# A long convolution and a state-space scan on one core: the convolution's transforms in smaller array pieces, with real and imaginary part on one partition, and a new order of all queues

## The chip, the cores and the metric

The kernel runs on one core of a Trainium2 chip. The metric is the device time of one launch in microseconds (us); lower is better. The core has five engines with a queue each: TensorE (PE in the profile, with its weight loads as a row of their own, PEld), VectorE (DVE), ScalarE (ACT), GpSimd (POOL) and SyncE (SP). Here POOL and SP do little but issue DMA transfers.

## The reference, cut to what matters

All inputs are bfloat16; S = 2048 positions, D = 1024 channels, L = 2S = 4096.

```python
# half A: gated long convolution            -> out[..., 0:1024]
k_shift = sum over t<4 of k_pad[:, t:t+S, :] * shift_k[:, 3-t]
kv  = k_shift * v
y   = irfft(rfft(pad(kv, L)) * rfft(pad(ssm_k, L)))[:S]    # along positions
out_a = q * (y + kv * ssm_D)

# half B: diagonal state-space model         -> out[..., 1024:2048]
dt = exp(log_dt);  Lam_bar = exp(dt * Lam)                 # complex, 1024 states
Bu = x @ (((Lam_bar - 1)/Lam)[:, None] * B).T
h[t] = Lam_bar * h[t-1] + Bu[t]
out_b = 2 * real(h @ C.T) + x * Dskip
```

## The kernel before

Everything is written out by hand. A string `ORDER` lists some 1,200 small tasks; the loop at the end of `full_kernel` runs them in that order, so that each engine's queue holds its share of the tasks in the order of the string. A word is a task with its arguments; `:a3` names the buffer slot that its result takes, and `@G`, `@S`, `@D` put a DMA on POOL's or SP's queue or a copy on DVE. No scheduler moves anything afterwards: a task that isn't ready holds up all that stands behind it on its engine.

Half B runs in 16 chunks i of 128 positions. B is loaded in 16 pieces (`bl`), turned on TensorE (`bT`, L458) and copied to `BT` by ACT or DVE (`bc`, L473 or L469). `x` (L483) and `cx` (L480) are transposing DMAs. `U.i.jp.jl` (L492) makes Bu in 16 matmuls of 128 columns; four `ue.i.jp` (ACT, L497) copy it out. Then DVE does, per chunk: `r1` (multiply by a rotating table, L506), `r2` (add, L518), `sc` (the scan, L523), `cm` (carry to the next chunk, L528), `r3` (L506) and `r4` (L535). `y.i.dh.part` (L546, and L551 for the skip) multiplies by C; `ye` (ACT, L556) and `yst` store it.

Half A is a 4096-point transform in two stages, through DRAM between them:

- `kp`, `vp` load k and v; `kvm`, `kva`, `kvb`, `kvc` (DVE, L583 to L604) make two rows of kv at a time.
- Stage 1: a 64-point transform over 128 partitions that hold two interleaved groups of 64 positions. The matrix `F1t` is padded with zeros to 128 x 128, so `am.r.u` (L610, two matmuls of 512 columns) does one half u of the frequencies for both groups; `ae` (ACT, L615) and `ast` store to `Ys_kv`. For the filter, `hl` loads, `hT` (L630) turns eight blocks on TensorE, `hc` (L635) copies, `hm.f.rp.u` (L643) is the matmul, `he` (L650) and `hst` store to `Ys_h`.
- Stage 2, for 16 groups gq: `lh`, `lk` load 512 KB each; `sh`, `sk` (L676) are 64 x 64 pieces, four of them in the array at a time; `she`, `ske` (ACT, L685, L691) copy to `hab` and `x16`. The real part stands on one 32-partition block and the imaginary part on the next. `sw` exchanges them: four SBUF-to-SBUF DMAs of 32 partitions. Then `pr` (DVE, L704) multiplies both forms by the k side, `sa` (L717, 64 x 64 pieces again) transforms back, `sae` (ACT, L724) and `vst` store to `Vs`.
- Last stage: `vl` and `qp` load, `a3.r` (L744, four matmuls with a padded `Gt`), `a3e` (ACT, L749), `qm` (multiply by q, DVE, L753), `ost`.

PSUM is eight banks: `p0`, `p1` (one bank each) and `d0` to `d2` (two banks each). The pool `a1` (k ring, filter taps) is closed when the convolution input is done, and `a2` (slots `a11` and up, `hab`) takes its place.

Of the kernel before, what the change touches and what calls it, by code (L numbers as in the profile page):

```python
# [16 lines left out]
BF16 = mybir.dt.bfloat16  # L17
# [5 lines left out]
NR = 16  # L23
# [4 lines left out]
def a_constants():  # L28
# [3 lines left out]
    F1 = np.zeros((64, 2, 2, 2, 2, 32))  # L32
    G1 = np.zeros((2, 2, 32, 2, 64, 2))
    for h in range(2):
        F1[:, h, :, h] = np.transpose(F, (0, 2, 1, 3))
        G1[h, :, :, :, :, h] = np.transpose(F, (1, 3, 2, 0)) * (2 / NFFT)
# [5 lines left out]
    WF = np.zeros((2, N2, 2, 32, 3, N2))  # L42
# [3 lines left out]
    WF[:, :, :, :, 2, :] = WF[:, :, :, :, 0, :]  # L46
    WI = np.zeros((2, 2, N2, 16, 2, 2, N2, 2))
    for gi in range(2):
        for ui in range(2):
            for gq in range(16):  # L50
                cc = np.transpose(c_[ui, 2 * gq + gi], (1, 0)); ss = np.transpose(s_[ui, 2 * gq + gi], (1, 0))
                o = WI[gi, :, :, gq, ui]
                o[0, :, 0, :, 0] = cc; o[0, :, 0, :, 1] = ss
                o[1, :, 0, :, 0] = -cc; o[1, :, 0, :, 1] = -ss
                for cp in range(2):
                    o[cp, :, 1, :, 0] = -ss; o[cp, :, 1, :, 1] = cc
    W = np.concatenate([WF.reshape(128, NWP, 4 * 96), WI.reshape(128, NWP, 2 * 256)], axis=2)
# [9 lines left out]
ld_par bl.4.0@G:b0 bl.5.0@G:b1 bl.5.1@G:b2 bl.4.1:b3 bl.6.0:b4 bl.2.1@G:b5 ld_sd@S bl.1.1@G:b6 ld_w@S:a0a1 kp.0@G kp.-2 ld_F par_T:p0 hl.2@G:a2  # L67
bl.7.0:b7 bT.4.0:p1 p32 exp1 bl.6.1:b8 hl.3@G:a3 bc.4.0 dve2 x.0:b9 kp.-1@G bT.5.0:p0 dve3 sm_pre bT.4.1:p1 bc.5.0 hl.1@G:a4 bl.0.1:b10 bc.4.1
bl.7.1@G:b11 x.4:b12 bT.6.0:p0 tabA1:a5a6a7a8 bc.6.0 bl.2.0:b13 hl.0:a9 exp2 bl.0.0:b0 sin0 rt@G kp.1 bT.1.1:p1 x.2:b1 bT.5.1:p0 tabA2 bc.1.1 cx.4.1
wb.7:p1 bc.5.1 par_rest vp.0@G:a10 ld_G@S sin2 wb.4:p0 cx.5.1 wbe.4 sin1 wb.6:p0 cx.0.0 wbe.6@D eo.0 bl.3.1:b3 wb.1:p0 wbe.7@D bl.1.0:b4 wbe.1@D  # L70
wb.2:p1 cx.0.1 eo.1 stt.0 wb.0:p0 cx.7.0 wbe.2 stt.1 eo.3 wb.5:p1 bl.3.0:b6 x.1:b2 wbe.5@D wbe.0 stt.3 wb.3:p1 wbe.3 bT.6.1:p0 cx.1.0 dd bT.2.0:p1
kvm.0:m0 vp.1:a1 vp.2:a0 cx.6.0 bc.6.1 cx.6.1 bT.0.1:p0 bc.2.0 bc.0.1@D kp.2@G eo.2 bT.2.1:p1 kva.0 hT.0.0:p0 hc.0.0:b8 stt.2 bc.2.1 hT.0.1:p0
bT.7.1:p1 hc.0.1:b13 kvb.0:a7 bc.7.1 hT.0.6:p0 hm.0.0.1:d0 kvc.0 hc.0.6:b10 hT.0.3:p1 hm.0.0.0:d1 kvm.4:m0 he.0.0.1:b5 am.1.1:d2 hc.0.3:b11
hm.0.6.1:d0 hst.0.0.1 hT.0.2:p0 bT.0.0:p1 he.0.6.1:b8 hc.0.2:b0 hst.0.6.1@S cx.1.1 bc.0.0 bT.7.0:p0 bc.7.0@D cx.3.1 z1 U.0.3.0:p1 kva.4 hm.0.6.0:d0
U.0.3.1 cx.3.0 U.0.2.0:p0 kvb.4:a8 U.0.2.1 ue.0.3:a10 he.0.6.0:b7 kvm.2:m0 bT.1.0:p1 bc.1.0 am.0.1:d0 bT.3.0:p1 ue.0.2 bc.3.0 bT.3.1:p0 bc.3.1
U.0.0.0:p1 U.0.0.1 he.0.0.0:b5 kp.4@G kva.2 kp.3@G ae.0.1:b10 hm.0.3.1:d1 U.2.2.0:p0 ue.0.0 ast.0.1@S vp.4:a5 kvc.4 U.0.1.0:p1 ae.1.1:b4 cx.5.0
hm.0.1.0:d0 he.0.3.1:b6 ast.1.1 kvb.2:a6 hm.0.3.0:d2 hst.0.6.0 U.0.1.1 he.0.1.0:b3 hst.0.3.1 kvc.2 U.2.2.1 ue.0.1 hst.0.1.0 he.0.3.0:b11 U.1.2.0:p1
r1.0:m0 ue.2.2:a0 hst.0.3.0@S hm.0.1.1:d1 hst.0.0.0@S am.4.0:d0 he.0.1.1:b8 cx.2.0 U.2.1.0:p0 r2.0:a1 U.1.2.1 U.2.1.1 ue.1.2:a10 kvm.8:m0 U.1.1.0:p1
ue.2.1 ae.4.0:b13 hm.0.2.0:d2 am.4.1:d1 z2 ast.4.0 am.0.0:d0 U.2.3.0:p0 hst.0.1.1 ae.4.1:b4 U.1.1.1 he.0.2.0:b7 ast.4.1@S sc.0 U.2.3.1 ue.1.1
hst.0.2.0@S hm.0.2.1:d1 cx.7.1 ue.2.3 am.5.1:d2 ae.0.0:b6 hT.0.4:p1 cx.2.1 am.2.0:d0 hc.0.4:b10 ast.0.0 U.1.0.0:p0 ae.2.0:b3 hT.0.7:p1 cx.4.0 kva.8  # L80
U.1.0.1 ue.1.0 hT.0.5:p0 hc.0.7:b0 hl.5:a9 kvb.8:a4 hl.4:a2 U.2.0.0:p1 hc.0.5:b13 ast.2.0@S hl.7:a3 r3.0:m0 U.1.3.0:p0 he.0.2.1:b8 am.1.0:d0 hst.0.2.1
hm.0.5.0:d1 U.1.3.1 cm.0:a7 kvc.8 U.2.0.1 ue.1.3 he.0.5.0:b11 r4.0 U.4.0.0:p0 ue.2.0 hm.0.4.0:d1 r1.1:m0 U.4.0.1 he.0.4.0:b5 U.4.2.0:p1 ue.4.0:a5
hst.0.4.0@S ae.5.1:b6 hm.0.7.1:d1 r2.1 U.4.2.1 ae.1.0:b4 ast.5.1 U.4.1.0:p0 hl.6@G:a10 r1.2:m0 he.0.7.1:b7 ast.1.0@S hst.0.5.0 am.8.1:d2 ue.4.2
U.4.1.1 hm.0.5.1:d0 sc.1 am.5.0:d1 he.0.5.1:b8 U.4.3.0:p1 ue.4.1 am.2.1:d0 ae.5.0:b3 y.0.0.0:p0 ae.2.1:b13 hm.0.4.1:d1 hm.0.7.0:d0 ast.2.1@S U.4.3.1
x.3:b6 he.0.7.0:b10 r2.2:a0 am.8.0:d0 ae.8.1:b5 hst.0.7.0 y.0.0.1 r3.1:m0 hst.0.5.1 ue.4.3 ast.8.1@S ast.5.0@S y.0.0.2 ae.8.0:b0 vp.3:a8 y.0.1.0:p1
ast.8.0 cm.1 hst.0.7.1 r4.1 am.3.0:d2 y.0.1.1 ae.3.0:b4 r1.4:m0 y.0.0.3 ast.3.0 ye.0.0:b11 hT.1.4:p0 y.0.1.2 sc.2 hc.1.4:b13 he.0.4.1:b10 hT.1.3:p0
# [60 lines left out]
def full_kernel(ctx, tc, A_q, A_k, A_v, A_shift_k, A_ssm_k, A_ssm_D, B_x, B_Lre, B_Lim, B_Bre, B_Bim,  # L147
# [96 lines left out]
    def k8(name, shape):  # L244
        return rtile(ap_pool("a2"), "e", name, shape)
# [578 lines left out]
```

## Time and profile before

| | before |
|---|---|
| time, median of 3 runs | 381.52 us (376.89, 381.52, 382.91) |
| span of the profiled execution | 378.5 us; no run time of its own is given for it, so the 3.0 us between span and median stands for what lies around the span |
| PE busy | 346.6 us (92%), 3661 matmuls |
| DVE busy | 324.6 us (86%), 229 instructions |
| ACT busy | 264.2 us (70%), 341 instructions |
| POOL busy | 81.3 us (21%) |
| DMA | 100.06 MB, mean 264 GB/s, 67418 packets |

How to read it: a busy share is an average over stages with different limits. Matmuls are pipelined, and the profile models their ends, so one that streams 512 columns is shown as about 380 ns long though the next starts sooner; what counts is the distance from start to start. "Idle before, releaser" says how long an engine stood still ahead of a group and what it waited for. In the timeline, a row merges neighbours of one kind: start, length, how many.

### The profile page before, as it was taken

How to read it: one execution, taken by the hardware profiler on the slowest of the kernel's cores; microseconds unless marked ns; L12 is line 12 of the kernel's file. 1: busy time of each engine (PE TensorE's matmuls, PEld its weight loads, DVE VectorE, ACT ScalarE, POOL GpSimd, SP SyncE). 2: the span in 40 equal slices, each digit the busy share in tenths (PEclk: the TensorE clock that was granted, in tenths of full speed). 3: DMA queues.
4: the chain of work that ended last, by engine and by line, in shares of the span. 5: the costliest groups of instructions: out<-in, count | busy, mean ns of one | idle time of the engine just before them, and what ended most of it. 6: DMA issues, size and time to landing. Idle time of an engine off the chain costs nothing.

```text
span 378.5 us, 8748 instructions
## 1 busy us (share of the span) xinstructions
PE 346.6 (92%) x3661; PEld 225.6 (60%) x3661; DVE 324.6 (86%) x229; ACT 264.2 (70%) x341; POOL 81.3 (21%) x150
## 2 busy tenths in 40 slices
PE   4548889899899999999999999989999999999995
PEld 3226678785455578855444757367867664467442
DVE  6989599999999997999997797576899999993972
ACT  4978798877778886952785879778869771346433
POOL 7300023022112521214200325330210202211021
PEclk9999999999999999999999999999999999999999
DMA  6999999997578999999999897999989539877995
GB/s 231 317 338 216 265 272 286 296 314 235 200 243 270 247 313 287 281 272 268 190 275 312 258 324 234 220 267 221 284 236 312 175 125 325 306 229 255 350 319 206
DMA packets 67418, 100.06 MB, mean 264 GB/s; under 512 B 38435, under 2 KB 42147, under 8 KB 67380
## 3 DMA queue, kind: packets, MB, share of 16 engines
q1 hardware_dynamic: 54660, 56.32, 54.8%
q0 software_dynamic: 12720, 43.19, 36.8%
q8 instruction: 28, 0.46, 0.5%
q14 instruction: 10, 0.08, 0.1%
HBM read 49.16 MB, written 33.55 MB: 219 GB/s over the span
## 4 chain that ended last, share of the span: by engine, by line
PE 56%; DMA 15%; issue 13%; ACT 7%; SPq 4%; POOL 2%; DVE 1%; POOLq 0%; ACTq 0%; DVEq 0%
PE ps_u L492 22%; PE ps_y L546 16%; PE ps_a L744 4%; DMA wts<-a_c_W 4%; SPq L483 4%; DMA Ys_kv<-ysb 3%; PE ps_a L643 3%; DMA l2k<-Ys_kv 3%; DMA ld<-in_B_B_re_dram 3%; PE ps_a L717 3%; PE ps_a L610 3%; DMA hab<-hab 2%; PE ps_a L676 2%; PE ps_t L630 2%; ACT ysb L615 2%
## 5 line engine op out<-in xcount | busy, mean ns | idle before, releaser
L492 PEld LDWEIGHTS <-BT 128*128 128x128 bf16 x2048 | 119.3, 98 | 22.6 <-issue 11.7
L492 PE MATMUL ps_u<-xT,BT 128*128 128x128 bf16 x2048 | 127.7, 219 | 2.4 <-ACT u L497 1.2
L546 PE MATMUL ps_y<-CT,h 128*128 128x512 bf16 x512 | 127.7, 379 | 0.0
L546 PEld LDWEIGHTS <-h 128*128 128x128 bf16 x512 | 44.6, 98 | 48.0 <-issue 6.1
L523 DVE TENSOR_TENSOR_SCAN h<-rtab,h 128x2080 bf16<-128x2080 f32 x16 | 71.8, 4488 | 0.2
L497 ACT CAST u<-ps_u 128x512 bf16<-128x512 f32 x64 | 38.2, 603 | 27.0 <-PE ps_u L492 19.1
L506 DVE TENSOR_TENSOR mt<-u,Z 128x4096 bf16<-128x4096 bf16 x16 | 36.7, 2291 | 15.8 <-ACT u L497 15.4
L704 DVE TENSOR_TENSOR hab<-x,hab 128x4096 bf16<-128x4096 bf16 x16 | 36.5, 2286 | 15.2 <-DMA hab<-hab 10.5
L556 ACT CAST yo<-ps_y 128x512 bf16<-128x512 f32 x32 | 19.1, 596 | 28.0 <-PE ps_y L546 24.4
L650 ACT CAST ysbh<-ps_a 128x1024 bf16<-128x1024 f32 x32 | 32.3, 1033 | 8.8 <-PE ps_a L643 7.5
L691 ACT CAST x<-ps_a 128x1024 bf16<-128x1024 f32 x32 | 31.9, 1026 | 8.8 <-PE ps_a L676 5.9
L506 DVE TENSOR_TENSOR mt<-h,Z 128x4096 bf16<-128x4096 bf16 x16 | 36.7, 2292 | 0.5
L724 ACT CAST vsb<-ps_a 128x1024 bf16<-128x1024 f32 x32 | 31.7, 1027 | 6.5 <-PE ps_a L717 6.0
L583 DVE TENSOR_TENSOR mt<-kring,wbc 128x2048 bf16<-128x2048 bf16 (+3 forms) x14 | 35.8, 2592 | 0.4 <-ACT wbc L473 0.2
L615 ACT CAST ysb<-ps_a 128x1024 bf16<-128x1024 f32 x32 | 32.3, 1043 | 2.7 <-issue 1.6
L685 ACT CAST hab<-ps_a 128x1024 bf16<-128x1024 f32 x32 | 32.2, 1030 | 2.1 <-PE ps_a L676 1.9
L551 PE MATMUL ps_y<-Dd,xT 128*128 128x128 bf16 x128 | 28.0, 219 | 0.0
L749 ACT CAST ot<-ps_a 128x1024 bf16<-128x1024 f32 x16 | 15.7, 1018 | 14.1 <-PE ps_a L744 14.1
L169 POOL DMA_DIRECT2D Ys_h<-ysbh x20 | 14.3, 716 | 43.3 <-ACT ysbh L650 43.3
L168 POOL DMA_DIRECT2D hab<-hab x32 | 15.6, 494 | 32.1 <-ACT hab L685 18.3
L458 PE MATMUL ps_t<-ident,ld 128*128 128x128 bf16 x128 | 13.9, 285 | 9.1 <-DMA ld<-in_B_B_re_dram 4.4
L643 PE MATMUL ps_a<-hT,F1t 128*128 128x512 bf16 x64 | 20.6, 402 | 0.8 <-ACT ysbh L650 0.6
(116 smaller groups left out, 381.8 us busy)
## 6 DMA issues: line engine op xcount, KB each, us to landing
Ys_h<-ysbh POOLq DMA_DIRECT2D x20, 256.0 KB, 5.5
l2h<-Ys_h SPq DMA_DIRECT2D x9, 512.0 KB, 9.7
Vs<-vsb SPq DMA_DIRECT2D x9, 512.0 KB, 4.3
vv<-Vs SPq DMA_DIRECT2D x9, 512.0 KB, 5.2
Ys_kv<-ysb POOLq DMA_DIRECT2D x17, 256.0 KB, 6.2
l2k<-Ys_kv SPq DMA_DIRECT2D x8, 512.0 KB, 3.9
hab<-hab SPq DMA_DIRECT2D x32, 128.0 KB, 5.4
l2k<-Ys_kv POOLq DMA_DIRECT2D x8, 512.0 KB, 7.8
```

Of the source, the lines that this page charges most:

```text
L492: nc.tensor.matmul(pu[:, w, jl, :], BT[:, 2 * jp + jl, w, d, :], xT[:, d, :], start=(d == 0), stop=(d == ND - 1))
L497: nc.scalar.copy(u[:, :, 2 * jp:2 * jp + 2, :], st["pu", i, jp][:])
L506: nc.vector.tensor_mul(m, s_, w_)
L523: nc.vector.tensor_tensor_scan(gf, rtab[:].rearrange("p a j t -> p (a j t)"), gf, 0.0, ALU.mult, ALU.add)
L546: nc.tensor.matmul(py[:], h[:, 1 - w, j, 2:TP], CT[:, j, w, dh * 512:(dh + 1) * 512], start=(j == 0 and w == 0), stop=(j == NJ - 1 and w = ...
L583: nc.vector.tensor_mul(m[:, :, j0:j0 + n, :], a_, wbc[:, j0:j0 + n, :].unsqueeze(1).to_broadcast([P, 2, n, DV]))
L615: nc.scalar.copy(st["ysb", r, u][:], st["pa", r, u][:].rearrange("p e d -> p (e d)"))
L643: nc.tensor.matmul(pd[:, e, :], F1t[:, u, :], st["hT", f, rp][:, e, :], start=True, stop=not sk)
L650: nc.scalar.copy(st["yh", f, rp, u][:], st["pa", f, rp, u][:])
L685: nc.scalar.copy(hab[:, a, :, e * 512:(e + 1) * 512], st["ps", key, gq, e][:])
L691: nc.scalar.copy(x16[:, :, e * 512:(e + 1) * 512], st["ps", "k", gq, e][:])
L704: nc.vector.tensor_mul(hab, x16.unsqueeze(1).to_broadcast([P, 2, 2 * D]), hab)
```

## The change

The matrices lose their zero padding. Each transform now runs in smaller pieces of the array that lie side by side, real and imaginary part of one frequency come out on the same partition (in two column ranges) rather than on two blocks of partitions, and positions are split over the partitions by the parity of the row of 16 (partitions 0 to 63 even, 64 to 127 odd).

- `am`, `hm`: two matmuls of 64 rows x 128 columns, one on each half of the rows, instead of two full ones: half as many columns are streamed if the two run at once.
- `hT`: 16 transposes of 64 columns rather than 8 of 128. `a3`: two pieces of 64 columns at a time, no accumulation.
- `sh`, `sk`: eight pieces of 64 x 32 per task, one group instead of two groups of four. `sa`: one task per gq, 32 pieces of 32 x 64 in four groups of eight, into two PSUM tiles.
- `sw` and its 64 DMAs are gone. `pr` takes both operands by broadcasting and writes a tile of its own.
- Loads and stores by rows become two DMAs of 64 partitions (`halves`, `l2`, `vst`, `ost`); `ast` is one DMA of 512 KB per r rather than two of 256 KB. `qm` is 8 multiplications of 2048 elements rather than 16 of 1024.
- DMAs that are issued: SP 187 before, 175 after; POOL 138 before, 141 after. Matmuls: 3661 before, 4299 after.
- `ORDER` is new throughout. Among other things, nine of the sixteen `BT` copies are on DVE (two before), two of the eight `wbe` copies (four before), and `rt` is on ACT (POOL before); the first `r1` stands behind 14 `he` (7 before), and most `cx` behind the first scans. `mt` is a smaller tile once `a2` is open, so `a` has 15 slots, `hab` two instead of three.

```diff
-    F1t = const.tile([P, 2, P], BF16, name="F1t")
-    Gt = const.tile([P, 2, P], BF16, name="Gt")
+    F1t = const.tile([P, P], BF16, name="F1t")
+    Gt = const.tile([P, 64], BF16, name="Gt")
...
+    def halves(o_, i_):
+        for h in range(2):
+            spd(o_[64 * h:64 * h + 64], i_[h])
...
-    def am(r, u):
+    def am(r, e):
         pd = dtile("ps_a")
-        for e in range(2):
-            nc.tensor.matmul(pd[:, e, :], F1t[:, u, :], kvt(r)[:, r % 2, e * 512:(e + 1) * 512], start=True, stop=True)
+        for h in range(2):
+            hp = slice(64 * h, 64 * h + 64)
+            nc.tensor.matmul(pd[:, h, :], F1t[hp, :], kvt(r)[hp, r % 2, e * 512:(e + 1) * 512], start=True, stop=True,
+                             tile_position=(64 * h, 0))
...
     def l2(nm, Ys, gq):
         st[nm, gq] = k4(nm, [P, 2, D])
-        spd(st[nm, gq][:], Ysv(Ys, gq))
+        for u in range(2):
+            spd(st[nm, gq][64 * u:64 * u + 64], Ysv(Ys, u, gq))
...
-        for gi in range(2):
-            for u in range(2):
-                up = slice(64 * u, 64 * u + 64)
-                nc.tensor.matmul(pd[64 * gi:64 * gi + 64, u, :], wt[up, b0:b0 + 64],
-                                 st[nm, gq][up, gi, e * 512:(e + 1) * 512], start=True, stop=True,
-                                 tile_position=(64 * u, 64 * gi))
+        for e in range(2):
+            for gi in range(2):
+                for u in range(2):
+                    up = slice(64 * u, 64 * u + 64)
+                    x = 32 * (2 * (u ^ gi) + e)
+                    nc.tensor.matmul(pd[x:x + 32, u, :], wt[up, b0:b0 + 32],
+                                     st[nm, gq][up, gi, e * 512:(e + 1) * 512], start=True, stop=True,
+                                     tile_position=(64 * u, x))
...
-    def sw(gq):
-        hab = st["hab", gq]
-        for b in range(4):
-            o = b ^ 1
-            spd(hab[32 * b:32 * b + 32, 1, :, :], hab[32 * o:32 * o + 32, 0, :, :])
...
     def pr(gq):
-        nc.vector.tensor_mul(hab, x16.unsqueeze(1).to_broadcast([P, 2, 2 * D]), hab)
+        st["m2", gq] = rtile(ap_pool("a2"), "e", "hab", [P, 2, 2, D])
+        nc.vector.tensor_mul(st["m2", gq][:], st["x16", gq][:].unsqueeze(2).to_broadcast([P, 2, 2, D]),
+                             st["h16", gq][:].unsqueeze(1).to_broadcast([P, 2, 2, D]))
...
+    def sa(gq):
+        wt, m = st["w", gq // 2], st["m2", gq]
+        pd = [dtile("ps_a") for _ in range(2)]
+        for n_, (a, b, wi) in enumerate(((0, 0, 0), (1, 1, 1), (0, 1, 2), (1, 0, 2))):
+            for e in range(2):
+                for s in range(2):
+                    for u in range(2):
+                        x = 32 * (2 * s + e)
+                        nc.tensor.matmul(pd[s][64 * u:64 * u + 64, e, :], wt[x:x + 32, b0:b0 + 64],
+                                         m[x:x + 32, a, b, u * 512:(u + 1) * 512], start=(n_ == 0), stop=(n_ == 3),
+                                         tile_position=(x, 64 * u))
...
-        for e in range(2):
-            for u in range(2):
-                nc.tensor.matmul(pd[:, e, :], Gt[:, u, :], st["vv", r][:, u, e * 512:(e + 1) * 512], start=(u == 0), stop=(u == 1))
+        for e in range(2):
+            for h in range(2):
+                nc.tensor.matmul(pd[64 * h:64 * h + 64, e, :], Gt[:], st["vv", r][:, h, e * 512:(e + 1) * 512],
+                                 start=True, stop=True, tile_position=(0, 64 * h))
```

More of the change, by code (lines that the diff above doesn't have):

```diff
@@ L71 @@
[L71 to L74, printed above, removed]
```

341 lines of the change are left out of this document (167 added, 174 removed).

## The prediction

> **What bounds the kernel now.** I read the page's busy shares first, then the busy time by stretches, cut where the fifth scan (chunk 4) starts and where the last `r4` ends.
>
> ```profile
> span 378.5 us, 8748 instructions
> PE 346.6 (92%) x3661; PEld 225.6 (60%) x3661; DVE 324.6 (86%) x229; ACT 264.2 (70%) x341; POOL 81.3 (21%) x150
> ```
> ```profile
> core 0: us, PE busy (x) PEld busy (x) DVE busy (x) ACT busy (x) POOL busy (x), PEclk, DMA share, GB/s
> 0.00:60.00 60.00, 40.56 (x377) 29.28 (x378) 50.21 (x79) 46.62 (x72) 15.73 (x34) 1.00 1.05 269
> 60.00:157.70 97.70, 93.81 (x1043) 67.37 (x1041) 93.09 (x50) 76.56 (x95) 22.95 (x37) 1.00 0.93 275
> 157.70:362.60 204.90, 200.12 (x2184) 123.42 (x2182) 175.10 (x93) 135.95 (x170) 39.35 (x74) 1.00 0.90 258
> 362.60:378.50 15.90, 12.05 (x64) 5.55 (x61) 6.24 (x11) 5.03 (x7) 3.25 (x6) 1.00 0.74 267
> ```
>
> Two halves. Up to 157.7 us DVE is the bound: it works 93 of the 98 us of the second stretch, and in the first it waits 10 us while loads arrive. PE's 94 are no peak, since its rows overlap. After 157.7 it is PE: 200 of 205 us, while DVE stands still for 30. So what PE loses in work counts only in the second half, and what DVE gains in work counts in the first. To make PE's work exact I take start-to-start distances from the timeline of PE, the critical chain, and PE's last row.
>
> ```profile
> 206.78 1.06 PE L492 MATMUL ps_u<-xT,BT 128*128 128x128 bf16 x16
> 207.77 1.06 PE L717 MATMUL ps_a<-hab,wts 64*64 64x512 bf16 x16
> 208.66 0.39 PE L676 MATMUL ps_a<-l2h,wts 64*64 64x512 bf16 x4
> 208.98 3.19 PE L492 MATMUL ps_u<-xT,BT 128*128 128x128 bf16 x54
> ```
> ```profile
> 336.84 1.73 PE ps_a L744 x8
> 338.56 0.89 PE ps_u L492 x16
> ```
> ```profile
> 370.82 3.83 PE L546 MATMUL ps_y<-CT,h 128*128 128x512 bf16 x17
> ```
>
> The 54 matmuls of 128 columns take 3.19 with a last one of 0.22, so one every 0.056. Eight of 512 columns take 1.72 to the next start: 0.215. Sixteen small pieces take 207.77 to 208.66, 0.89: four groups of four, 0.22 per group, as long as one full matmul. And a change of the array's form costs something: 16 x 0.056 is 0.90, but from the `U` run at 206.78 to the pieces at 207.77 it is 0.99, so 0.09. Back again: 0.32 for one group, 0.22 plus 0.10. I take 0.094 per change.
>
> What PE has to do behind 157.7 us, by group:
>
> ```profile
> L546 PE MATMUL ps_y<-CT,h 128*128 128x512 bf16 x416 | 102.8, 379 | 0.0
> L492 PE MATMUL ps_u<-xT,BT 128*128 128x128 bf16 x1154 | 72.8, 219 | 1.0 <-ACT u L497 1.0
> L551 PE MATMUL ps_y<-Dd,xT 128*128 128x128 bf16 x104 | 22.8, 219 | 0.0
> L717 PE MATMUL ps_a<-hab,wts 64*64 64x512 bf16 x256 | 18.2, 383 | 0.8 <-DVE hab L704 0.7
> L744 PE MATMUL ps_a<-vv,Gt 128*128 128x512 bf16 x64 | 16.1, 379 | 0.0
> L676 PE MATMUL ps_a<-l2k,wts 64*64 64x512 bf16 x128 | 10.8, 385 | 0.0
> L676 PE MATMUL ps_a<-l2h,wts 64*64 64x512 bf16 x120 | 10.7, 386 | 3.0 <-DMA wts<-a_c_W 2.3 <-DMA l2h<-Ys_h 0.7
> L610 PE MATMUL ps_a<-acc,F1t 128*128 128x512 bf16 x4 | 1.2, 382 | 0.0
> ```
>
> That is 416 x 0.215 = 89.4 for `y`, 1258 x 0.056 = 70.4 for `U` and the skip, 126 groups of four x 0.22 = 27.7, 68 full matmuls x 0.215 = 14.6: 202.1. `ORDER` has 75 changes of form behind `sc.4`: 7.1. Sum 209.2. PE ends at 374.7, 217.0 after the scan began: it waits 7.8 us in this half, no more.
>
> **The change part by part.** *PE's second half.* `ORDER` of the changed kernel, behind `sc.4`: `y` is unchanged (104 tasks, 89.4). `U` has 62 tasks instead of 72, since ten more stand ahead: 992 + 104 matmuls x 0.056 = 61.4. 57 `sh`/`sk` tasks are a group of eight pieces each, 16 `sa` four groups each: 121 groups. No row shows eight pieces at once. Below, a group costs the 0.22 of a group of four; above, twice that, if only four run at a time. I take 0.22: the sixteen pieces above follow without loss. 26.6. `a3` is 32 pairs of 64-column pieces instead of 64 full matmuls: 6.9 at 0.215, 13.8 if they don't pair; I take the pair, by the same row. 184.3 in all, and 93 changes of form, 8.7: 193.0. **Term 1: 193.0 - 209.2 = -16.2**, of which 9.0 is `U` moved forward, 6.9 `a3`, 1.9 sections that are finished earlier, and 1.6 is paid back in changes of form.
>
> The halved `am` and `hm` (64 full matmuls each, now 32 pairs: 2 x 6.9 us) lie ahead of `sc.4`, as do most of 101 added changes of form (190 against 89 by the built order, +9.5 in all). They cost or bring nothing of their own there, because DVE is the bound; what they do is make room for the ten `U`. If that cover fails, term 1 loses up to its 9.0. [...]
>
> *DVE's first half.*
>
> ```profile
> L469 DVE COPY BT<-ps_t 128x1024 bf16<-128x1024 bf16 x2 | 1.4, 692 | 5.8 <-PE ps_t L458 5.8
> L469 DVE CAST wbc<-ps_a 128x512 bf16<-128x512 f32 x4 | 2.7, 688 | 0.4 <-PE ps_a L409 0.3
> L753 DVE TENSOR_TENSOR ot<-ot,qt 128x1024 bf16<-128x1024 bf16 x16 | 10.2, 686 | 3.4 <-ACT ot L749 2.7 <-DMA qt<-in_A_q_dram 0.7
> L602 DVE TENSOR_TENSOR acc<-mt 128x2048 bf16<-128x2048 bf16 x8 | 9.8, 1224 | 0.8 <-PE ps_t L630 0.5
> ```
>
> Seven more `BT` copies, two fewer `wbe`: 7 x 0.69 - 2 x 0.69 = 3.5 us on the engine that sets this half's end. **Term 2: +3.5.** `qm` goes from 10.2 to 8 x 1.22 = 9.8, late, off the path. `pr` keeps its 4096 elements, and L506, which broadcasts likewise, is as fast:
>
> ```profile
> L506 DVE TENSOR_TENSOR mt<-u,Z 128x4096 bf16<-128x4096 bf16 x16 | 36.7, 2291 | 15.8 <-ACT u L497 15.4
> L704 DVE TENSOR_TENSOR hab<-x,hab 128x4096 bf16<-128x4096 bf16 x16 | 36.5, 2286 | 15.2 <-DMA hab<-hab 10.5 <-ACT x L691 4.6
> ```
>
> *The start.* The first `r1` needs all of `u` of chunk 0.
>
> ```profile
> 57.62 0.58 ACT L497 CAST u<-ps_u 128x512 bf16<-128x512 f32 x1
> 58.10 1.02 ACT L650 CAST ysbh<-ps_a 128x1024 bf16<-128x1024 f32 x1
> 59.00 0.60 ACT L497 CAST u<-ps_u 128x512 bf16<-128x512 f32 x1
> ```
> ```profile
> 58.23 2.29 DVE L506 TENSOR_TENSOR mt<-u,Z 128x4096 bf16<-128x4096 bf16 x1
> ```
>
> The last of them ended at 58.20. On ACT, `ORDER` now puts eight more `he`, two more `ae`, three more `hc`, two more `wbe` and the two copies of `rt` ahead of it, and takes seven `bc` away: 6 x 0.9 (58.10 to 59.00, start to start) + 2 x 0.6 (512 columns, as `u`) + 2 x 0.9 (1024 elements, as `ysbh`) = about 8.4 us more. ACT stands idle for 13.4 of the first 60 us, waiting for loads, so part of it is absorbed; DVE itself comes 2 us later (seven copies more, two casts and one `kvc` less). Between 0 and +7 for DVE's wait; I take the lower middle because most of the transposing `cx` loads, and their traffic, have left this stretch. **Term 3: +3.** Behind this wait stands everything on DVE.
>
> *Exchange, DMAs.* `sw` was waited for by DVE, 10.5 us, in the half where DVE has 30 us to spare; PE waited 0.7 for `hab`. So its removal brings PE between 0 and 2 us. The split loads and stores add issues, the exchange takes 64 away (SP 187 to 175, POOL 138 to 141): nothing, and if queues did fall behind, `lk` would be late and `sk` with it. **Term 4, PE's own waits: 0**, between -4 and +8: DVE's work in this half is 181, PE's was 209 and will be 193, so their distance shrinks from 28 to 12 and each holds up the other more often; against that, the exchange is gone.
>
> Sum: 378.5 - 16.2 + 3.5 + 3 = 368.8 us span. The median of the three runs lies 3.0 above the span, so 371.8; I predict **372**, 2.5% faster. 2% is about what a measurement of this kernel can tell from no change; its edges are 373.9 and 389.2.
>
> **The rivals.**
>
> 1. *Eight pieces don't run at once.* For: nothing in the trace shows more than four, and eight need their instructions issued twice as fast, eight pairs in 0.22 us against one pair per 0.056 now. Against: groups of four follow at the length of one full matmul. Four at a time cost 121 x 0.22 = +26.6 behind `sc.4`: **398**, slower. Half-way, 0.33 per group, is +13: 385. It eats the whole gain from 0.30 per group (9.7 / 121 = 0.08). [...]
> 2. *The start takes the gain.* If ACT absorbs none of the 8.4 us and `kvm` waits for its later loads too, DVE's half ends 10 rather than 3 us later: **379**, no change. For: DVE waited 10 us there already. Against: less traffic.
> 3. *PE's waits vanish* and the start costs nothing: 372 - 3 - 7.8 = **361**. For: 2.3 of the waits are for `wts`, now ordered anew. Against: DVE is closer behind.
> 4. *PSUM.* `sa` takes two of the three `d` tiles at once, and each has to be copied out by ACT before the next `sk` or `sh` can start. One copy (1.02 us in the ACT rows above) exposed at each of 16 `sa`: +16.3, **388**. Against: ACT works 136 of 205 us in this half, and `ORDER` puts `U` and `y` between.
>
> **How the numbers follow.** Forecast 0.43, rival 1 0.15, rival 2 0.20, rival 3 0.12, rival 4 0.10. From the forecast's bounds (366 to 377) a seventh falls in "within 2%"; of rival 1 and rival 4 more than half are slower by over 2%, of rival 2 a fifth. Faster 0.48, same 0.28, slower 0.24. The range goes from 358, below rival 3, to 394, which leaves out the four-at-a-time case: 358 to 394.
>
> **What would show it.** Right: groups of eight start 0.22 apart; `a3` pairs 0.215; first `r1` at 61 to 65 us; the fifth scan at about 164; PE busy nearly throughout behind it, and DVE's idle time there below 20 us. Wrong: groups of eight 0.3 or more apart; the fifth scan later than 170; PE rows with idle time ahead of `sk`, released by ACT `vsb`.

## The result, and the profile after

The changed kernel is slower: 414.9 us (median of four runs, 406.6 to 424.6) against 382.2 for the kernel before; the ratio is 1.079, with a 95% interval from 1.060 to 1.098. The prediction was 372, with 358 to 394. Ratios, and spans that are compared below, rest on undisturbed runs, and so does the range given at the end for the kernel before; where a kernel had too few of them for a ratio, its times stand alone.

The profiled execution took 412.6 us, 410.9 of it span: 32.4 us more span than before. From its page:

```profile
span 410.9 us, 9906 instructions
PE 341.3 (83%) x4265; PEld 222.5 (54%) x4299; DVE 324.9 (79%) x226; ACT 262.0 (64%) x338; POOL 83.5 (20%) x151
q1 hardware_dynamic: 52820, 49.05, 49.2%
q0 software_dynamic: 12480, 42.00, 35.1%
```

The engines' busy time hardly changed (DVE 324.6 before, ACT 264.2), so all that was lost is idle time. The last two rows hold the surprise: packets, MB, and share of the 16 DMA engines' span. Before, they read

```profile
q1 hardware_dynamic: 54660, 56.32, 54.8%
q0 software_dynamic: 12720, 43.19, 36.8%
```

Before, 99.5 MB on these two queues took 91.6% of 378.5 us, 346.7; after, 91.1 MB took 84.3% of 410.9, 346.4. The exchange's 8.4 MB are gone and nothing was saved: each MB takes 9% more of the engines' time (3.80 us against 3.48).

By stretches, cut like the prediction's (first `r1`, fifth scan, last `r4`; the columns are as there):

```profile
0.00:69.60 69.60, 41.36 (x436) 28.69 (x436) 48.13 (x82) 52.69 (x79) 19.50 (x42) 0.93 0.99 235
69.60:178.10 108.50, 92.52 (x1206) 72.84 (x1207) 96.09 (x52) 69.16 (x87) 19.72 (x31) 0.94 0.95 241
178.10:382.60 204.50, 189.03 (x2527) 112.81 (x2555) 173.49 (x89) 131.62 (x162) 36.65 (x65) 0.99 0.75 204
382.60:410.90 28.30, 18.41 (x102) 8.19 (x101) 7.25 (x6) 8.52 (x11) 7.65 (x13) 0.94 0.86 264
```

The first `r1` comes at 70.0 instead of 58.2 (+11.8), the fifth scan at 178.1 instead of 157.7 (+20.4 in all), and from there to the end it takes 232.8 instead of 220.8 (+12.0). So two thirds of the loss lie in the half where the forecast had +6.5, and the other half lost 12 where it was to gain 16. Up to the fifth scan the DMA engines have no room: their share is 0.99 and 0.95, and DVE stands still for 33.9 us. Behind it their share fell (0.75 in the long stretch, 0.90 before), but single loads come late there.

Share times length also says why an equal total is no draw. Up to the fifth scan the engines work 172 us for 42.5 MB (GB/s times length), against 154 us for 43.0 MB before; behind it 178 against 196. The exchange's saving lies behind the scan, where the engines had more room, and most of the higher price per MB is paid ahead of it (4.05 us against 3.58 there, 3.61 against 3.43 behind it).

PE's waits behind the fifth scan, by line, what was waited for, us, times, longest (1.8 us of `issue` left out):

```profile
PE ps_a L744 <- DMA vv<-Vs: 8.0, 5, 2.7
PE ps_a L686 <- DMA wts<-a_c_W: 3.0, 3, 2.3
PE ps_a L686 <- DMA l2h<-Ys_h: 1.9, 2, 1.2
PE ps_u L488 <- ACT yo L552: 1.9, 1, 1.9
PE ps_a L686 <- DMA l2k<-Ys_kv: 0.6, 1, 0.6
PE ps_a L686 <- ACT vsb L721: 0.2, 1, 0.2
```

Four of these six are loads, 13.5 us together. The largest stalls ahead of the scan are in the timelines of PE, DVE and ACT (start, length, and in brackets the idle time before with its releaser):

```profile
40.32 1.03 PE L454 MATMUL ps_t<-ident,ld 128*128 128x128 bf16 x8 [8.04 <-DMA ld<-in_B_B_im_dram]
161.31 6.43 PE L488 MATMUL ps_u<-xT,BT 128*128 128x128 bf16 x80 [8.75 <-ACT u L493]
```
```profile
151.33 1.23 DVE L605 TENSOR_TENSOR acc<-acc,v 128x2048 bf16<-128x2048 bf16 x1 [3.41 <-DMA v<-in_A_v_dram]
152.47 2.28 DVE L502 TENSOR_TENSOR mt<-u,Z 128x4096 bf16<-128x4096 bf16 x1
154.67 4.48 DVE L519 TENSOR_TENSOR_SCAN h<-rtab,h 128x2080 bf16<-128x2080 f32 x1
159.25 0.30 DVE L524 TENSOR_TENSOR h<-h,AB 128x32 bf16<-128x32 bf16 x1
159.37 1.23 DVE L514 TENSOR_TENSOR h<-mt 128x2048 bf16<-128x2048 bf16 x1
```
```profile
160.67 1.07 ACT L493 CAST u<-ps_u 128x512 bf16<-128x512 f32 x2 [12.57 <-DVE h L514]
```

The first is a load of B that came late. The second stall is read through three engines: DVE waits 3.4 us for a load of v; the row at 152.47 is `r1.3`, but its second half `r2.3` (159.37) stands behind the scan `sc.2` (154.67); `r2.3` frees the slot that ACT's `ue` needs; ACT stands 12.6 us, and PE, without room for `U`, 8.75.

### The profile page after: what moved, and what is told of

Its sections match the earlier page's. It is cut to its first block, busy times and chain, and to the rows that moved or that the text cites. A ratio compares the mean times of both kernels' runs of the same rounds, so it can differ in the third digit from the quotient of the medians.

```text
span 410.9 us, 9906 instructions
## 1 busy us (share of the span) xinstructions
PE 341.3 (83%) x4265; PEld 222.5 (54%) x4299; DVE 324.9 (79%) x226; ACT 262.0 (64%) x338; POOL 83.5 (20%) x151
## 5 line engine op out<-in xcount | busy, mean ns | idle before, releaser
L488 PE MATMUL ps_u<-xT,BT 128*128 128x128 bf16 x2048 | 129.7, 222 | 14.8 <-ACT u L493 11.1
L488 PEld LDWEIGHTS <-BT 128*128 128x128 bf16 x2048 | 120.7, 99 | 32.4 <-issue 26.6
L542 PE MATMUL ps_y<-CT,h 128*128 128x512 bf16 x478 | 123.1, 381 | 4.8 <-DMA CT<-in_B_C_im_dram 1.8
L542 PEld LDWEIGHTS <-h 128*128 128x128 bf16 x512 | 43.7, 98 | 54.3 <-issue 17.3
L493 ACT CAST u<-ps_u 128x512 bf16<-128x512 f32 x64 | 37.4, 595 | 42.5 <-PE ps_u L488 26.0
L700 DVE TENSOR_TENSOR hab<-x,h 128x4096 bf16<-128x4096 bf16 x16 | 36.5, 2287 | 26.0 <-ACT x L694 21.1
L694 ACT CAST h<-ps_a 128x1024 bf16<-128x1024 f32 x32 | 31.7, 1028 | 4.2 <-PE ps_a L686 3.5
L634 PE MATMUL ps_t<-ident,hk 128*64 128x128 bf16 x256 | 17.4, 286 | 6.8 <-DMA hk<-in_A_ssm_k_dram 5.5
L634 PEld LDWEIGHTS <-hk 128*64 128x64 bf16 x256 | 16.0, 203 | 10.2 <-DMA hk<-in_A_ssm_k_dram 6.2
L754 DVE TENSOR_TENSOR ot<-ot,qt 128x2048 bf16<-128x2048 bf16 x8 | 9.7, 1224 | 14.9 <-ACT ot L750 9.0
```

Of the source, the lines that this page charges most:

```text
L488: nc.tensor.matmul(pu[:, w, jl, :], BT[:, 2 * jp + jl, w, d, :], xT[:, d, :], start=(d == 0), stop=(d == ND - 1))
L493: nc.scalar.copy(u[:, :, 2 * jp:2 * jp + 2, :], st["pu", i, jp][:])
L542: nc.tensor.matmul(py[:], h[:, 1 - w, j, 2:TP], CT[:, j, w, dh * 512:(dh + 1) * 512], start=(j == 0 and w == 0), stop=(j == NJ - 1 and w = ...
L634: nc.tensor.transpose(pt[64 * h:64 * h + 64, e, b * P:(b + 1) * P], hv[:, 2 * rp + e, h, :], ident[:], tile_position=(0, 64 * h))
L694: nc.scalar.copy(t_[:, c_, :], st["ps", key, gq, c_][:].rearrange("p e d -> p (e d)"))
L700: nc.vector.tensor_mul(st["m2", gq][:], st["x16", gq][:].unsqueeze(2).to_broadcast([P, 2, 2, D]), st["h16", gq][:].unsqueeze(1).to_broadca ...
```

## The experiments

Two theories stood against each other: *the pieces* (they don't run side by side, or drain the array) and *the order* (the new queues and slots). A third, *the split transfers*, came later, out of the rows of the queues above. "The order searched" below means an `ORDER` written by a program that shuffles tasks, queues and slots and lets a model of in-order queues, with durations from the profiles, judge each.

**Pieces or order: each with the other's partner**

```diff
 # e1: the changed functions with the words of the old ORDER, slots dealt anew
-ORDER = """ld_w@S:a2a0 wb.3:p0 wbe.3 wb.6:p1 wbe.6 hl.3@G:a3 ...
+ORDER = """ld_par bl.4.0@G:b0 bl.5.0@G:b1 bl.5.1@G:b2 bl.4.1:b3 ...
 # e2: the old functions with the words of the new ORDER, slots dealt anew
-ORDER = """ld_par bl.4.0@G:b0 bl.5.0@G:b1 bl.5.1@G:b2 bl.4.1:b3 ...
+ORDER = """ld_w@S:a0a1 wb.3:p0 wbe.3 wb.6:p1 wbe.6 hl.3@G:a2 ...
```

> The changed kernel's tasks (small pieces, no exchange, parity halves, split loads and stores) put in the order of the kernel before; slots dealt out anew, the one least recently freed first, and a hundred of 1174 tasks a few places later where no slot is free. Theory O (the new order of the queues cost the time, the pieces did what they should): PE's work behind the fifth scan falls by the 6.9 us of the halved last stage and a little more, nothing is lost at the start, so 368 to 378 us; up to 385 if the untuned slots cost something; fifth scan at 155 to 163 us. Theory P (the pieces or their layout cost the time: two d tiles at once for the inverse stage, split transfers, changes of form): 400 to 420 us whatever the order.

> The other corner: the matrices, the exchange and the transfers of the kernel before, with its tasks put in the changed kernel's order (slots dealt out by the same rule; the exchange stands right behind the two copies that it needs). Theory O: 400 to 430 us, with the first r1 at 65 us or later and PE standing still at the same places. Theory P: 375 to 392 us, as the kernel before.

Measured: 443.2 us (ratio 1.167, 1.155 to 1.179) and 573.0 (1.505, 1.493 to 1.517). Both misses: tasks and slots don't fit each other across designs, and the slots that were dealt anew made waits of their own. They tell nothing of either theory.

**Three repairs of single waits**

```diff
 # e3: the two early cx, transposing loads of C that take 4.19 and 5.72 us on SP's queue, go behind the first scan
-... wb.1:p1 wbe.1 cx.3.0 bT.4.0:p0 ... he.0.4.0:b1 bT.1.0:p0 cx.1.0 bc.1.0 ...
+... wb.1:p1 wbe.1 bT.4.0:p0 ... he.0.4.0:b1 bT.1.0:p0 bc.1.0 ... he.1.3.1:b0 cx.3.0 cx.1.0 cx.0.1 ...
 # e4: a third slot (b13) for the weights of stage 2, each lw one place earlier
-... lw.0@S:w1 ... lw.1@G:w0 ... lw.3@G:w1 ... lw.2@G:w0 ...
+... lw.0@S:w0 lw.1@G:w1 ... lw.3@G:b13 ... lw.2@G:w0 ... lw.4@S:w1 ...
 # e7: r2.3 ahead of the scan that it stood behind
-... r1.3:m0 sc.2 cm.2:a9 ue.10.1:a8 lw.0@S:w1 am.13.1:d2 r2.3 ...
+... r1.3:m0 ue.10.1:a8 lw.0@S:w1 am.13.1:d2 r2.3:a9 sc.2 cm.2 ...
```

> The changed kernel with the two early transposing loads cx.3.0 and cx.1.0 moved behind, ahead of cx.0.1; nothing else. Theory S (these transposes hold the DMA engines while a B load of 256 KB takes 13 us, and PE, ACT and DVE stand still from 36 to 40 us for it): first r1 at 60 to 63 instead of 69.6 us, and 405 to 409 us in all. Rival (the load traffic as a whole is the limit of the start, whatever its order): first r1 still at 67 to 71, 413 to 417 us.

> The changed kernel with three slots for the stage-2 weights instead of two (the third in b13, which is free behind the first stage; x.11 and ye.11.0 take other b slots), and each weight load in the place of the one before it. The chain shows three waits for these weights, 5.7, 3.0 and 5.0 us. Theory W (each of them is what ended last): 401 to 408 us. Rival (behind each the next wait, for a vsb store or a late k load, ends soon after): 411 to 417 us.

> The changed kernel with one change in DVE's queue: r2.3 ahead of sc.2 and cm.2, so that the last user of the closing pool (its product tile) ends one scan earlier. Theory Q (ACT's 12.6 us wait of ue.7.0 for that pool, and PE's 8.7 behind it, set the fifth scan): 3 to 5 us faster, 406 to 410 us. Rival (the late v load ahead of it sets that stretch, and DVE has the same work to do anyway): 412 to 416 us.

> The changed kernel with the two repairs together, the third weight slot and r2.3 ahead of the scan. If the two waits lie one behind the other (each is a stall of its own), the gains of the two runs add, 9 and 5 us: 399 to 402 us. If one hides the other: 405 to 409 us.

Measured: e3 420.2 us (1.101, 1.090 to 1.111): the first `r1` came 6 us earlier, at 63.7, but the fifth scan 4 later, at 182.4; a miss. e4 409.5 (1.073, 1.064 to 1.083), span 404.7: the waits for `wts` are gone. e7 405.9 (1.071, 1.058 to 1.084), span 405.3: PE's stall shrank as it should,

```profile
153.89 7.21 PE L488 MATMUL ps_u<-xT,BT 128*128 128x128 bf16 x80 [3.97 <-ACT u L493]
```

from 8.75 to 3.97. Each spared some 6 us of span, and neither ratio leaves the interval of the changed kernel. e10, both at once, ran from 399.0 to 417.7: inconclusive. The waits are real, but they don't add up to 32 us, and what e3 repaired at the start came back ahead of the fifth scan.

**The order searched**

```diff
-ORDER = """ld_w@S:a2a0 wb.3:p0 wbe.3 wb.6:p1 wbe.6 hl.3@G:a3 ...
+ORDER = """hl.3@G:a4 ld_F@G bl.6.0@G:b0 bl.4.0@G:b6 hl.1@S:a1 ...      (e5)
+ORDER = """hl.1@G:a3 bl.1.0@G:b6 bl.6.0@S:b13 bl.4.0@G:b9 hl.2@G:a0 ... (e6)
+ORDER = """bl.1.1@G:b0 bl.4.0@S:b9 bl.2.1@S:b8 bl.3.1@S:b6 ld_par ...   (e8)
+ORDER = """bl.2.1@G:b1 bl.1.0@S:b0 bT.1.0:p1 hl.2@S:a6 bl.4.0@S:b4 ...  (e9)
```

> The changed kernel with the same tasks, pieces, layout and memory, in another order: positions in the queues, slots, and which queue issues a DMA (SP or POOL) or makes a wbe or bc copy (ACT or DVE) were searched with a model that has the durations of the profile and in-order queues. Theory O (order alone costs the 32 us): 365 to 385 us, PE's waits behind the fifth scan below 12 us. Theory P (the pieces or their layout): 400 us or more, since no piece, transfer or copy is changed.

> The same as the run before, from another start of the search; its model has the fifth scan at 153 instead of 159 us. Theory O: 363 to 385 us. Theory P: 400 us or more.

> The changed kernel's tasks, pieces and memory in a third searched order; the model now also holds back SP while its transposing loads drain (they move 138 GB/s in the trace, plain ones 290 to 330), and each load of k waits for all readers of the rows that it overwrites. The model says 372, and 391 with DMAs a tenth slower. Theory O (the order alone costs the time): 372 to 392 us, fifth scan at 160 to 175 us, PE's waits behind it under 8 us. Theory P (pieces or layout): 400 us or more.

> The same with another result of the search (model 373 and 390 us). Theory O: 372 to 392 us. Theory P: 400 us or more.

In e5 and e6 one load of rows of k stands ahead of the last reader of the rows that it overwrites, so a few rows of the convolution use other rows of k. Measured: e5 406.4 us (1.073, 1.060 to 1.086); e6 398.8, one run at 388.4; e8 383.1 (1.014, 1.007 to 1.020), span 382.1; e9 391.3 (1.026, 1.015 to 1.037). So the order carries much: e8 has the same work and the same transfers and is 25 us faster than the changed kernel by the ratios, 29 by span. Its two queues still take 90.4% of 382.1 us, 345.4 us of the 16 engines and as much as the changed kernel's 346.4: the transfers cost the same there, and this order stands still less for it. But even e8 only comes near the kernel before, though the model gave it 372; its fifth scan starts at 168.8, later than the 157.7 of before.

**The split transfers**

The pairing by parity makes seven kinds of transfers two of 64 partitions each. e11 makes them one of 128 again, in the changed kernel's own order; the rows then meet wrong partners, so its convolution isn't the reference's, with the same work and bytes. e14 does so for the scratch transfers alone (`l2`, `vst`; its convolution is likewise another). e13 keeps the split and takes rows in sequence instead of by parity (again another convolution). e15 is the kernel *before*, its loads and the store `vst` split, with the same rows in the same places. e12 is e11's edit in e8's order.

```diff
 # e11 (and e12), kernel after
-    kr, vr, qr, oar = (a_.rearrange("(n h s) d -> h n s d", h=2, s=NR) for a_ in (k, v, q, out_a))
+    kr, vr, qr, oar = (a_.rearrange("(n s) d -> n s d", s=NR) for a_ in (k, v, q, out_a))
...
-        for u in range(2):
-            spd(st[nm, gq][64 * u:64 * u + 64], Ysv(Ys, u, gq))
+        spd(st[nm, gq][:], Ysv(Ys, gq))
...
 # e13, kernel after
-            spd(o_[64 * h:64 * h + 64], i_[h])
+            spd(o_[64 * h:64 * h + 64], i_[64 * h:64 * h + 64])
...
 # e15, kernel before
+    def halves(o_, i_, q_=spd):
+        for h in range(2):
+            q_(o_[64 * h:64 * h + 64], i_[64 * h:64 * h + 64])
-        spd(st["v", r][:], vr[:, 2 * r:2 * r + 2, :])
+        halves(st["v", r][:], vr[:, 2 * r:2 * r + 2, :])
...
```

> The changed kernel, same order and pieces, with every transfer that it splits into two halves of 64 partitions (loads of k, v, q, of both stage-1 results, stores of the inverse stage and of the output) as one transfer of 128 partitions again. The positions are then not the reference's (rows of 16 in sequence instead of by parity), so the output differs; bytes and work are the same. Theory D (halves of 64 partitions are slower or block the issuing queues, so loads come later than the order allows for): 385 to 400 us. Theory O (the order's own waits): 405 to 420 us, as before the edit.

> The same edit in the best searched order (run e8, 383.1 us). Theory D: 370 to 378 us, with the first r1 at 63 us or earlier instead of 68. Theory O: 380 to 388 us.

> The changed kernel with its split kept, two transfers of 64 partitions each, but with the rows that the unsplit run e11 moved (rows of 16 in sequence; output not the reference's). Theory D1 (two transfers of 64 partitions are slower than one of 128): 405 to 418 us and 4 KB packets as slow as in the changed kernel (161 ns on SP's queue, 224 on POOL's). Theory D2 (the addresses by parity are what is slow): 385 to 395 us and packets as in e11 (139 and 194 ns).

> The changed kernel with only the scratch transfers of stage 2 (lh, lk, vst: 48 transfers) unsplit, k, v, q and the output split as it has them (rows of the scratch in another sequence, output not the reference's). Theory D, if every split transfer costs alike: about six tenths of e11's 26 us, so 397 to 402 us. If the loads of the start are what counts: 405 to 412 us; if stage 2 is: 390 to 395 us.

> The kernel before, unchanged but for its loads of k, v, q and of both stage-1 results and the store of the inverse stage, which are each done as two transfers of 64 partitions, on the same queue at the same place. Theory D1: 390 to 405 us, packets of 4 KB slower by 10 to 15%. Theory D2 (parity addresses) or O (order): 376 to 385 us.

e11: 388.6 us (386.6 to 390.4; ratio 1.032, 1.023 to 1.041, clear of the changed kernel's interval). Its page:

```profile
span 387.9 us, 9773 instructions
q1 hardware_dynamic: 52180, 49.05, 45.2%
q0 software_dynamic: 11824, 41.99, 32.1%
```

The same MB now take 77.3% of 387.9, 299.8 us of the 16 engines instead of 346.4, and the span is 23.0 shorter. By the ratios it is 4.7% of the time before, 18 us. The loads of B on POOL's queue, which are not split in either kernel, paid for it (KB each, median us from issue to landing; the changed kernel, then e11):

```profile
ld<-in_B_B_re_dram POOLq DMA_DIRECT2D x5, 256.0 KB, 12.2
```
```profile
ld<-in_B_B_re_dram POOLq DMA_DIRECT2D x5, 256.0 KB, 6.4
```

Those of the imaginary part went from 9.7 to 4.9 there; the few on SP's queue did not gain (5.7 to 6.9, 3.7 to 3.8). The first `r1` of e11 stands where the prediction had it, between 61 and 65:

```profile
61.69 2.29 DVE L502 TENSOR_TENSOR mt<-u,Z 128x4096 bf16<-128x4096 bf16 x1 [0.42 <-ACT u L493]
```

Its fifth scan starts at 164.8; the prediction said about 164. Up to there:

```profile
0.00:61.70 61.70, 39.33 (x444) 28.07 (x445) 47.99 (x83) 52.77 (x80) 17.13 (x38) 1.00 0.90 274
61.70:164.80 103.10, 89.74 (x1210) 70.53 (x1212) 95.92 (x52) 68.45 (x86) 16.87 (x26) 0.95 0.92 248
```

The engines work 150 us for the same 42.5 MB, instead of 172. The second stall is not the split's: PE of e11 still has it, 10.9 us long and released by ACT's `u` at 148.5.

e14: 409.4 us (1.069, 1.057 to 1.081), span 401.1:

```profile
q1 hardware_dynamic: 52372, 49.05, 47.6%
q0 software_dynamic: 12160, 42.00, 33.9%
```

81.5% of 401.1 is 326.9 us, 19.5 of the 46.6 that e11 saves, and 9.8 of its 23.0 us of span: four tenths of the dose, four tenths of the effect, by the span of one execution each. By its ratio alone e14 can't be told from the changed kernel. e13: 411.1 us, 404.3 to 416.2. With rows in sequence the time stays at the changed kernel's, far above e11's, so it is the two transfers and not the parity of the addresses. e15 (`ost` stays whole in it): 394.2 us (1.036, 1.024 to 1.048): the split alone makes the kernel before 3.6% slower, some 14 us, though nothing else in it changed. e12: 381.1 us, 374.3 to 385.4, beside e8's 383.1, and a span of 372.4 beside 382.1: where the order leaves loads more room, the split is worth between 2 and 10 us, and these runs don't settle which.

The traces' records of single packets say the same whatever the order. Of the 4 KB packets on SP's queue 21% took over 0.2 us in the kernel before and 14% in e11; 55% did in the changed kernel, 57% in e13, 60% in e15, and 28% in e14, where part of the split is left; in the searched order it is 45% split (e8) and 13% unsplit (e12). So the packets themselves are slower where transfers are split, in both designs and with either choice of rows. (The 161 and 224 ns in e13's expectation are the changed kernel's means over all packets of 2 KB and more; those of 4 KB alone have 245 and 220.)

**What is left, and the kernel before with its order searched**

e18 is e11 with the edits of e4 and e7 (its convolution is e11's, not the reference's); e16 and e17 are the kernel before with searched orders.

```diff
 # e18, on top of e11
-... r1.3:m0 sc.2 cm.2:a9 ue.10.1:a8 lw.0@S:w1 am.13.1:d2 r2.3 ...
+... r1.3:m0 ue.10.1:a8 lw.0@S:w0 lw.1@G:w1 am.13.1:d2 r2.3:a9 sc.2 cm.2 ...
 # e16, e17, kernel before
-ORDER = """ld_par bl.4.0@G:b0 bl.5.0@G:b1 bl.5.1@G:b2 bl.4.1:b3 ...
+ORDER = """bl.6.0@S:b3 ld_w@G:a4a9 bl.4.0@S:b6 bT.6.0:p0 hl.0@S:a3 ...   (e16)
+ORDER = """bl.1.1@S:b13 kp.-1@G bl.0.1@G:b2 bl.6.1@G:b8 bl.3.0@G:b0 ...  (e17)
```

> The changed kernel with unsplit transfers (as e11, output not the reference's) and the two repairs of e10, the third weight slot and r2.3 ahead of the scan. Theory: what e11 still has over the kernel before, 10 us, is the order's own waits, of which PE shows 20.5 us behind the fifth scan: 374 to 382 us. If these waits only hide others: 385 to 390 us.

> The kernel before with its own matrices, exchange and transfers, only its order, slots and queues searched in the way of e8 (durations of its own profile; the model gives it 382 as it stands and 367 for this order). If a searched order gains as much as the model says: 360 to 372 us, a version that beats both. If the order of before is as good as orders get on the chip: 375 to 385 us.

> The same from another start of the search (model 367): 360 to 372 us, or 375 to 385 us.

e18: 381.7 us (380.1 to 383.0, below every run of e11), span 379.6. Its last three stretches:

```profile
60.90:166.00 105.10, 93.24 (x1254) 72.43 (x1253) 96.34 (x52) 70.47 (x90) 18.15 (x28) 0.97 0.96 254
166.00:366.00 200.00, 195.22 (x2570) 114.84 (x2564) 176.98 (x91) 134.06 (x166) 24.94 (x42) 1.00 0.71 222
366.00:379.60 13.60, 8.77 (x48) 3.88 (x44) 3.59 (x3) 4.20 (x6) 2.01 (x3) 1.00 0.74 294
```

That closes the account of the spans, one execution each: 410.9 to 387.9 by the split (23.0), to 379.6 by the edits of e4 and e7 (8.3), and 1.1 is left to the 378.5 of before. The shares depend on the sequence: on top of the split, e4 and e7 brought some 6 us each by span and less by ratio. The second stall is shorter in e18 and not gone: PE still waits 7.6 us for ACT's `u`. e16: 372.9 us (369.7 to 374.3), span 370.8, beside 373.7 to 381.1 of the kernel before in all the sets of runs; e17: 382.6, 377.8 at best. So e16 is the fastest kernel here, ahead of the kernel before by about 1% and without an interval, and the old design with a searched order stands 10 us below the new design with one (e8). How they would stand without the split is not shown: e12's fastest run took 374.3.

## Why the prediction was wrong, point by point

**The step that failed** is the sentence "The split loads and stores add issues, the exchange takes 64 away ...: nothing". Transfers were counted by the issues on SP and POOL and by bytes; what the DMA engines need for them was not. Two halves of 64 partitions cost the 16 engines more than one of 128, 346.4 us against 299.8 for the same bytes, and as the half up to the fifth scan has no room in its DMA share (0.99 and 0.95), it came back as late loads: of B and v there, of `vv` behind it. How much of it becomes time hangs on the order: e8 pays the same on the engines and is 25 us faster. The sum had no term for it, no rival had it, and the range stopped short of it. The same sentence named `lk` as what would be late; the waits for `l2k` are 0.6 us, and `vv`, unsplit itself, is the longest.

The rival that was missing is that halves cost the engines more. That they do, e11 and e15 show: in the changed kernel all bytes together take 16% more of the engines' time than in e11 (346.4 / 299.8), and the same 99.5 MB take 382.1 us of it in e15 (96.6% of 395.6) against the 346.7 of the kernel before. Of the changed kernel's 91 MB, 42 are split (160 transfers of 256 KB), so it is about a third more on those, an estimate that takes every MB to cost the same unsplit. e13 leaves the addresses out as a cause. But a half is also a smaller transfer, and unsplitting takes issues away besides (POOL was busy for 83.5 us in the changed kernel, 61.9 in e11). Neither was tried apart (two transfers of 128 partitions and half the columns would do it), so which property of the halves costs stays open.

**Term 1** (-16.2). The prices held. The chain's rows (start, distance to the next, how many):

```profile
263.37 1.00 PE ps_a L714 x32
264.37 1.00 PE ps_u L488 x16
265.37 0.56 PE ps_a L686 x16
...
276.78 0.77 PE ps_a L686 x24
...
320.52 0.34 PE ps_a L686 x8
320.86 1.00 PE ps_a L714 x32
...
368.76 0.98 PE ps_a L744 x8
```

One, two and three groups of eight `sh`/`sk` pieces take 0.34, 0.56 and 0.77: 0.22 per group, and 0.12 for the change of form. The four groups of `sa` take 1.00, the same 4 x 0.22 + 0.12. Eight pieces do run at once, and rival 1 is dead. The four pairs of `a3` take 0.98, or 0.86 without the change: 0.215 each, as taken. Ahead of `sk` the 16 matmuls of `U` at 264.37 take 1.00 instead of 0.90, so a change costs 0.10 to 0.12 rather than 0.094, some 2 us over the 93 that the prediction counted. Four of those 93 are changes between two small forms; no row of the kernel before shows one, and the 0.094 that the sum takes for them was an estimate from the others. The one at 320.86 costs the same 0.12.

What failed is the count, which took PE to be level with `ORDER` when the fifth scan starts. PE's last row

```profile
400.21 3.83 PE L542 MATMUL ps_y<-CT,h 128*128 128x512 bf16 x17
```

puts its end at about 403.7 (the modelled end of the last matmul left out), 225.6 behind the scan. By the same prices the work in it is 203: the 193.0 of the prediction, 7.3 for eight `y` tasks that slid behind the scan (32 x 0.215 + 8 x 0.056; e18, whose records are complete, has 448 matmuls of `y` there where 416 were counted), 1.0 for 18 matmuls of `U`, and 1.5 for seven more groups. So the term is -6 instead of -16.2. The prediction saw the place, "if that cover fails, term 1 loses up to its 9.0", but not who pays: the ten `U` did move ahead of the scan, nearly whole, and `y` that `ORDER` has ahead of it fell behind it. In the kernel before `ORDER` and trace agree (104 tasks of `y` in both). That PE now stands still ahead of the scan (8.0 and 8.75 us) is the likely reason, not a shown one: e18, whose PE still stands 7.6 us there, has the same 448.

**Term 2** (+3.5) held for what it covered: the nine `BT` copies take 6.2 us (1.4 before) and the two `wbe` casts 1.4 (2.7 before). Up to the fifth scan DVE was busy for 48.13 + 96.09 = 144.2 us, against 50.21 + 93.09 = 143.3 before, only +0.9. The difference is chiefly one instruction of 128 x 8 (L329 before), which took 2.44 us and now takes 0.17. Before, POOL made the two copies of `rt` in just that time, and now ACT makes them; that they were what held it up is not shown. All the rest of the 20.4 us is DVE standing idle, 33.9 us instead of 14.4, and the two largest waits name what for:

```profile
L465 DVE COPY BT<-ps_t 128x1024 bf16<-128x1024 bf16 x9 | 6.2, 690 | 14.8 <-PE ps_t L454 14.8
L605 DVE TENSOR_TENSOR acc<-acc,v 128x2048 bf16<-128x2048 bf16 x8 | 9.8, 1222 | 6.9 <-DMA v<-in_A_v_dram 6.8
```

The first was 5.8 us before (its row is in the prediction), 6.2 in e11: the 8 to 9 us more are PE's wait of 8.0 for a load of B. The second was 0.7 before, 3.1 in e11 and 6.5 in e18, so the split alone does not explain it.

**Term 3** (+3, 0 to +7) was +11.8. e11 has +3.5 and e18 +2.7, so the term was right for what it covered (ACT's longer queue). Its reason for the lower middle, less traffic, did not hold: up to the first `r1` 16.4 MB were moved (69.6 us at 235 GB/s) and 16.1 before.

**Term 4** (0, -4 to +8) was about +15: 225.6 less 203 is some 22 us of waiting, against 7.8. PE's rows list 17.5 of them, and 8.0 + 3.0 + 1.9 + 0.6 are loads. In e18 the waits are back at 7: 208.4 us from the scan to PE's end, 201.5 of it work. No row shows a gain from the exchange's end, which was bounded at 0 to 2.

**What had no term.** Between the first `r1` and the fifth scan DVE needed 108.1 us instead of 99.5, +8.6, most of it the waits for v; and the tail behind PE's end grew by 3.4. With them the account closes: +11.8 and +8.6 up to the scan, -6.4, +15.0 and +3.4 behind it, 32.4 in all.

**Signs.** Groups, pairs: right. First `r1` at 61 to 65, scan at 164: wrong, but right as soon as the split is undone. DVE's idle time behind the scan: 31 us in the long stretch, not below 20. PE idle ahead of `sk` released by ACT `vsb`: 0.2 us, so rival 4 is out too. Rival 2 (the start takes the gain) came nearest in place, with a mechanism that it didn't have. Even e18, without the split and with both edits, has no gain: +8.3 up to the scan, where 6.5 was forecast, and -7.2 behind it instead of -16.2; of the 9.0 that are missing, the `y` that slid are 7.3. The halved transforms save PE's work in the half where DVE sets the end.

## What to carry to other kernels

Where the DMA share is near 1 (0.93 to 1.05 up to the fifth scan of the kernel before), price a transfer by the time of its packets on the engines, not by bytes and issues: a layout that makes one transfer of 128 partitions into two of 64 cost 14 us in a kernel in which nothing else changed. Before counting moved work as a gain, ask which engine has room for it: work that only moves ahead of a boundary needs an engine that is free there. And compare designs each with an order of its own; a transplanted order told nothing here.

## What the runs showed of the hardware

A PE that stood still for some 8 us was slow afterwards: eight transposes of B take 0.62 us ahead of the first stall (at 31.66) and 1.03 behind it (at 40.32). The granted clock in stretches of 5 us (eighth column) around the two stalls of the changed kernel:

```profile
35.00:40.00 5.00, 0.00 (x0) 0.00 (x0) 0.21 (x1) 1.39 (x5) 0.00 (x0) 0.54 0.90 85
40.00:45.00 5.00, 4.68 (x34) 3.02 (x35) 3.58 (x4) 2.64 (x3) 1.31 (x2) 0.50 1.01 241
45.00:50.00 5.00, 4.89 (x67) 4.04 (x64) 3.94 (x3) 4.46 (x6) 0.29 (x1) 0.93 0.81 228
...
155.00:160.00 5.00, 0.00 (x0) 0.00 (x0) 4.91 (x3) 0.00 (x0) 0.00 (x0) 0.50 0.63 201
160.00:165.00 5.00, 3.69 (x36) 3.69 (x36) 4.97 (x2) 2.91 (x4) 0.00 (x0) 0.50 0.27 75
```

PE is idle from 32.3 to 40.3 and from 152.6 to 161.3; both times the clock falls to 0.50 in the wait (at 35.4 and 154.9) and stays there for 5.3 and 3.8 us after work has come back, so that some 4.6 us are lost behind the stalls themselves, an estimate (half of 9.1). Length alone does not decide, though. The same trace has two shorter falls, to 0.50 for 3.4 us each: at the end of a gap of 2.3 us (145.8 to 148.2), and in the second of two of 1.2 and 0.8 us with a single matmul between them (193.6 to 196.0).

```profile
145.00:150.00 5.00, 2.69 (x26) 2.15 (x25) 2.81 (x2) 0.58 (x1) 0.00 (x0) 0.81 0.80 264
...
195.00:200.00 5.00, 4.16 (x34) 1.53 (x34) 0.98 (x1) 2.84 (x3) 0.00 (x0) 0.66 0.85 197
```

A gap of 2.7 us (361.3 to 363.9) left the clock at 1.00:

```profile
363.93 1.05 PE L744 MATMUL ps_a<-vv,Gt 128*64 128x512 bf16 x8 [2.66 <-DMA vv<-Vs]
```
```profile
360.00:365.00 5.00, 2.29 (x15) 0.87 (x15) 4.79 (x2) 1.01 (x1) 0.00 (x0) 1.00 1.00 270
```

The trace of the kernel before has records of the clock from 41.7 us on, all at 1.00 to the end of the span; PE's longest gap in that time is 1.8 us. Ahead of a trace's first record (28.6 us in the changed kernel) the view prints 1.00 too, but the rows of both traces show the slower rate there, 1.01 us for eight transposes of B, so the gaps in that time can't be judged:

```profile
32.84 1.01 PE L458 MATMUL ps_t<-ident,ld 128*128 128x128 bf16 x8
```

From what length of a gap on the clock falls is not shown here. Each of the four falls begins while PE already stands still, so none is the cause of the wait that it begins in.
